# Weight columns side by side in the second product of an attention and MoE kernel, and its last bank transposed apart

## Chip, core and metric

The kernel runs on one core of a Trainium2 chip. The metric is device time in microseconds (us) of one execution. Timed runs give a median; one more execution was profiled, and its trace is what the rows below come from.

## What is computed

```python
# q, k, v: (8, 8, 576, 64) float32; w_in: (512, 2048); w_out: (2048, 512)
scores = scale * np.matmul(q_c, k_c.transpose(0, 1, 2, 4, 3))   # in chunks of 64 rows, scale 1/8
scores = scores - np.max(scores, axis=-1, keepdims=True)
attn = np.exp(scores)
attn = attn / (np.sum(attn, axis=-1, keepdims=True) + 1e-09)
out = np.matmul(attn, v_c)
...
x = attn_out.transpose(0, 2, 1, 3).reshape(4608, 512)
h = x @ w_in
g = np.where(h >= 1, h, np.where(h <= -1, 0.0, (h + 1) ** 2 / 4))
result = g @ w_out
```

## The kernel before

Everything is computed to fp32 accuracy from fp32r products: each operand is split into a high and a low half, and a product is three matmuls (high x high, low x high, high x low) that add into one PSUM bank. The 4608 tokens lie in nine tiles of 512. The first three tiles go through the two feed-forward products directly (L625 first, L661 second). The other six go in **three pairs**, t = 3, 5 and 7, and each pair uses a seven-product scheme in place of eight block products: a whole stage (`whole_last`, matmuls at L918), where the hidden layer comes from P1 to P7, and an output stage (`both_out`, matmuls at L1124), where the second product comes from another set named P1 to P7. Chunk attention for later tiles is slipped between these products as bursts (L480 scores, L502 values).

**The output stage.** `OUT_ORDER` is P1, P2, P6, P5, P7, P3, P4; each has NQ = 8 steps, 56 steps a pair. A step takes one block of combined weights [128, 512] from a ring (`from_ring`; ten slots, filled from DRAM by DMAs on POOL's queue, `load_next_of_ring`) as its stationary operand, and one block of activations as its moving operand. The activations are prepared by `operand_of`: ACT casts the high half into one of 12 slots (L743), VectorE subtracts to get the low half (L747); some need a VectorE sum first. A step is six matmuls of 128 x 128 by 128 x 512, three into each of two banks. The first three don't need the low half until the third one.

Which bank takes which columns: the weight block is read as `"p (x d b) -> p x b d"`, so bank b gets the columns 2d + b, every second one. A result leaves transposed: VectorE's 32 x 32 transposes write both banks interleaved into one staging buffer (L1155), and four DMAs write rows of 64 floats, 256 bytes, to DRAM (`send`, L1163), on SP's queue, for the very last product two on SP's and two on ACT's.

**Banks.** `o_banks[2:]` are the two halves of one PSUM buffer, `ps_o23`; `o_banks[:2]` and `h_banks` are two separate buffers each. A reader of a buffer waits for all writes to that buffer that stand ahead of it. In each pair P1, P6, P7 and P4 run on the halves of `ps_o23`, P2 on `h_banks`, P5 and P3 on `o_banks[:2]`. The whole stage uses `h_banks` and `o_banks[:2]` in turn.

**The end.** For the last product of the last pair (P4) the last `LAST` = 3 steps are emitted together and bank by bank: all of bank 0, then all of bank 1.

**What sets the order.** Every piece is given to a `Plan` with an engine, a cost and its keys; `Plan.emit` walks a modelled time and emits the pieces in the order in which each engine would take them. So the order is fixed at build time, and each engine runs its own list in that order. DMAs from SP and ACT take eight semaphore lanes in turn (DMAHW0 to DMAHW7), and one that takes a lane waits until the DMA before it on that lane has landed. The staging buffers of a pair's first two sends are also the place of a later operand (`take_low`: `low`), which may be written once the sends have left.

The places that matter, L1085 and L1122:

```python
        banks = dict(zip(OUT_ORDER, (o_banks[2:], h_banks, o_banks[2:], o_banks[:2], o_banks[2:], o_banks[:2],
                                     o_banks[2:])))
...
                        w = ap().rearrange("p (x d b) -> p x b d", x=2, b=2)
```

## Time and profile before

| | us |
|---|---|
| median of 3 timed runs | 816.32 (814.77 to 816.89) |
| the profiled execution | 815.4 |
| its span in the trace | 813.6 |
| the output stages: first, second, third pair | 404 to 490, 571 to 653, 726 to 807 |

The span is what the trace covers, from the first to the last instruction. TensorE's granted clock is 0.998 of full over the span. Names in the rows: PE is TensorE's matmuls, PEld its weight loads (they run beside matmuls), DVE is VectorE, ACT ScalarE, SPq and ACTq are the DMA issues of SP and ACT. Buffers that were handed on show the name of the tile that lies there: `new_wi` and `new_wo` are places of former weights that hold the operands, blocks and ring slots of the pairs. A row of a timeline begins with its start and its length in us; neighbouring instructions of one form are merged, and their count stands behind the x.

### The profile page before, as it was taken

The numbers are of one execution on the slowest core, as the hardware profiler recorded it, in microseconds if no ns is written. First come the engines' busy times: TensorE is split into PE (matmuls) and PEld (weight loads), VectorE is DVE, ScalarE is ACT, GpSimd is POOL, SyncE is SP. The second block draws the span as 40 slices with busy tenths as digits, with TensorE's granted clock in tenths as the row PEclk, the third lists the DMA queues.
The fourth block names the chain that finished last, engine by engine and source line by source line (L and its number), as shares of the span: only waits on it lengthen the run. The fifth ranks groups of instructions, "written<-read, shape, count | busy, mean of one in ns | idle before, by whom it ended". The sixth has DMA issues, their size and how long they took to land.

```text
span 813.6 us, 16852 instructions
## 1 busy us (share of the span) xinstructions
PE 800.5 (98%) x5648; PEld 657.0 (81%) x5648; DVE 656.4 (81%) x1131; ACT 538.9 (66%) x1293; POOL 343.1 (42%) x606
## 2 busy tenths in 40 slices
PE   8999999999999999999999999999999999999996
PEld 7778778888888888888888888888888888888885
DVE  5899998768799996776999995877995845589851
ACT  5799876555577675687985655888854456685440
POOL 2112223575655464554554334554333333333330
PEclk9999999999999999999999999999999999999999
DMA  9999725887988897999999788977676886666773
GB/s 216 250 272 271 212 50 150 242 272 226 288 253 228 203 295 197 292 259 253 255 257 269 207 239 254 258 225 210 181 215 188 220 236 194 195 193 191 213 204 88
DMA packets 264149, 181.50 MB, mean 223 GB/s; under 512 B 217600, under 2 KB 229376, under 8 KB 264064
## 3 DMA queue, kind: packets, MB, share of 16 engines
q0 software_dynamic: 40640, 122.72, 48.3%
q1 hardware_dynamic: 220256, 56.92, 31.9%
q10 hardware_dynamic: 3168, 0.79, 0.5%
q8 instruction: 45, 0.74, 0.4%
q14 instruction: 40, 0.33, 0.1%
HBM read 133.17 MB, written 38.80 MB: 211 GB/s over the span
## 4 chain that ended last, share of the span: by engine, by line
PE 87%; DMA 4%; DVE 4%; SPq 4%; issue 1%; ACT 0%; DVEq 0%; ACTq 0%
PE ps_o L1124 25%; PE ps_o L918 14%; PE ps_h L918 14%; PE ps_o L661 13%; PE ps_h L625 13%; PE ps_h L1124 4%; PE ps_a L502 2%; DMA q_sb<-in_q_dram 2%; PE ps_a L480 2%; SPq L382 1%; DMA words<-in_moe_w_in_dram 1%; DVE parts L350 1%; SPq L368 1%; DMA k_sb<-in_k_dram 1%; SPq L388 1%
## 5 line engine op out<-in xcount | busy, mean ns | idle before, releaser
L743 ACT CAST new_wi<-new_wi 128x512 fp32r<-128x512 f32 x157 | 94.9, 626 | 64.8 <-PE ps_o L1124 34.7
L747 DVE TENSOR_TENSOR new_wi<-new_wi,new_wi 128x512 fp32r<-128x512 f32 (+2 forms) x191 | 122.1, 674 | 15.3 <-ACT new_wi L743 12.1
L625 PE MATMUL ps_h<-xh,parts 128*128 128x512 f32 x384 | 130.0, 398 | 2.6 <-DVE r L636 1.4
L661 PE MATMUL ps_o<-parts,gh 128*128 128x512 f32 x384 | 118.5, 390 | 0.0
L625 PEld LDWEIGHTS ps_h<-xh,parts 128*128 128x128 f32 x384 | 71.9, 188 | 19.5 <-DVE parts L350 2.1
L580 POOL DMA_DIRECT2D aT<-e x96 | 48.3, 510 | 87.3 <-ACT tmp L323 34.3
L661 PEld LDWEIGHTS ps_o<-parts,gh 128*128 128x128 f32 x384 | 71.9, 188 | 14.9
L661 PE MATMUL ps_o<-parts,gl 128*128 128x512 f32 x192 | 74.7, 389 | 0.0
L949 DVE SCALAR_TENSOR_TENSOR new_wi<-h,new_wi 128x512 f32<-128x512 f32 x63 | 42.3, 684 | 26.1 <-ACT new_wi L948 26.1
L547 ACT ACTIVATE e<-ps_a,mx 128x64 f32<-128x64 f32 x168 | 50.8, 327 | 10.5 <-DVE mx L541 5.4
L948 ACT ACTIVATE new_wi<-new_wi 128x512 f32<-128x512 f32 x84 | 51.2, 627 | 1.2
L945 ACT ACTIVATE new_wi<-h 128x512 f32<-128x512 f32 x63 | 39.5, 632 | 17.0 <-DVE h L939 17.0
L625 PE MATMUL ps_h<-x_parts,parts 128*128 128x512 f32 x128 | 50.1, 391 | 0.2 <-DVE x_parts L610 0.2
L644 ACT CAST gh<-r 128x512 fp32r<-128x512 f32 x48 | 29.9, 622 | 27.6 <-DVE r L636 19.5
L1124 PE MATMUL ps_o<-new_wi,new_wo 128*128 128x512 f32 x180 | 44.6, 394 | 0.0
L1124 PE MATMUL ps_o<-new_wi,ring_gh 128*128 128x512 f32 x168 | 43.8, 395 | 0.0
L1124 PE MATMUL ps_o<-new_wi,ring_gl 128*128 128x512 f32 x168 | 43.8, 395 | 0.0
L661 PEld LDWEIGHTS ps_o<-parts,gl 128*128 128x128 f32 x192 | 36.1, 188 | 7.5
L1124 PE MATMUL ps_o<-new_wi,ring_r 128*128 128x512 f32 x168 | 41.6, 394 | 0.0
L1124 PEld LDWEIGHTS ps_o<-new_wi,new_wo 128*128 128x128 f32 x180 | 34.7, 193 | 7.2
L1124 PE MATMUL ps_o<-new_wi,new_wi 128*128 128x512 f32 x162 | 40.4, 394 | 0.0
L747 DVE TENSOR_TENSOR new_wi<-new_wi 128x512 f32<-128x512 f32 (+2 forms) x64 | 39.5, 632 | 0.5
(229 smaller groups left out, 2034.4 us busy)
## 6 DMA issues: line engine op xcount, KB each, us to landing
ring_r<-combos POOLq DMA_DIRECT2D x36, 256.0 KB, 3.8
new_wo<-sums_P POOLq DMA_DIRECT2D x36, 256.0 KB, 3.1
new_wi<-combos POOLq DMA_DIRECT2D x34, 256.0 KB, 4.0
new_wi<-sums_P POOLq DMA_DIRECT2D x34, 256.0 KB, 3.2
ring_gh<-combos POOLq DMA_DIRECT2D x33, 256.0 KB, 4.1
ring_gl<-combos POOLq DMA_DIRECT2D x33, 256.0 KB, 4.3
ring_gh<-sums_P POOLq DMA_DIRECT2D x33, 256.0 KB, 3.4
ring_gl<-sums_P POOLq DMA_DIRECT2D x33, 256.0 KB, 3.4
```

The costliest lines, as they stand in the source:

```text
L547: nc.scalar.activation(out=e3[:, n, :], in_=sc[:, n // 4, n % 4, :], func=AF.Exp, bias=mx[:, n, :], scale=SCALE, accum_out=sm[:, n, :],)
L580: queues[queue].dma_start(out=aT[b:b + Q, to], in_=x[a:a + Q, of])
L625: nc.tensor.matmul(out=ps, lhsT=weight["wi", j][:, half, kc * P:(kc + 1) * P], rhs=x, start=(kc == 0 and i == 0), stop=(kc == KC - 1 and i ...
L644: plan.add("act", 0.52, lambda: nc.scalar.copy(out=gh, in_=now(r)), (rkey,), (ghkey, f"split_{t}_{j}"), ahead=ahead)
L661: nc.tensor.matmul(out=acc, lhsT=x[:, cols], rhs=weight["wo", j][:, half, :], start=(j == 0 and i == 0), stop=(j == NF - 1 and i == 2),)
L743: "act", cost, lambda: nc.scalar.copy(out=out(), in_=src()), reads, writes, ahead=ahead
L747: plan.add("dve", cost, lambda: nc.vector.tensor_tensor(out=out(), in0=one(), in1=two(), op=op), reads, writes, port=True, ahead=ahead)
L918: nc.tensor.matmul(out=ps, lhsT=w()[:, at:at + P], rhs=y(), start=name in FRESH and i == 0 and k == 0, stop=i == 1 and k == 2, skip_group_ ...
L945: plan.add("act", 0.52, lambda: nc.scalar.activation(out=now(r), in_=h(), func=AF.Relu, bias=0.5, scale=0.5), (hkey,), (rkey,), ahead=50)
L948: plan.add("act", 0.52, lambda: nc.scalar.square(out=now(r), in_=now(r)), (), (rkey,), ahead=50)
L949: plan.add("dve", 0.6, lambda: nc.vector.scalar_tensor_tensor(out=now(r), in0=h(), scalar=1.0, in1=now(r), op0=ALU.max, op1=ALU.min), (hke ...
L1124: nc.tensor.matmul(out=acc, lhsT=w[:, half, b], rhs=x(), start=name in alone and p == 0 and k == 0, stop=p == NQ - 1 and k == 2, skip_grou ...
```

## The change

- The weight block is read as `"p (x b d) -> p x b d"`: bank b gets the 128 columns b x 128 to b x 128 + 127, which lie side by side.
- So a bank holds whole output columns in one block, the transposes write each bank to its own contiguous half of the staging buffer, and a DMA writes rows of 32 floats, 128 bytes. A send is eight DMAs in place of four, four for each bank, and those of a bank depend on that bank's transpose alone.
- In the last pair P1, P6, P7 and P4 run on `h_banks` (two buffers), P2 on the halves of `ps_o23`. The other pairs keep their banks.
- `LAST` is 4: the last four steps of the last product go bank by bank.

```diff
-        banks = dict(zip(OUT_ORDER, (o_banks[2:], h_banks, o_banks[2:], o_banks[:2], o_banks[2:], o_banks[:2],
-                                     o_banks[2:])))
+        run, other = (h_banks, o_banks[2:]) if last else (o_banks[2:], h_banks)
+        banks = dict(zip(OUT_ORDER, (run, other, run, o_banks[:2], run, o_banks[:2], run)))
...
-                        w = ap().rearrange("p (x d b) -> p x b d", x=2, b=2)
+                        w = ap().rearrange("p (x b d) -> p x b d", x=2, b=2)
...
             for b, (key, ap) in enumerate(source):
-                plan.add("dve", 0.62, lambda b=b, ap=ap: nc.vector.transpose(
-                    out=turned().rearrange("p (n d b) -> p b n d", b=2, d=Q)[:, b],
-                    in_=ap().rearrange("p (n d) -> p n d", d=Q),
-                ), (key,), (keys[b],), ahead=0 if last else -40)
-            for n, queue in enumerate(queues_of):
-                def emit(n=n, queue=queue):
+                plan.add("dve", 0.62, lambda b=b, ap=ap: nc.vector.transpose(out=room_of()[:, b, :], in_=ap()),
+                         (key,), (keys[b],), ahead=0 if last else -40)
+
+                def emit(n, queue, b=b):
                     for a in range(n, P // Q, len(queues_of)):
-                        d = half * QC + a * 2 * Q
+                        d = half * QC + b * P + a * Q
                         queues[queue].dma_start(
-                            out=out[row:row + T, d:d + 2 * Q].rearrange("(n p) d -> p n d", p=Q),
-                            in_=turned()[a * Q:(a + 1) * Q].rearrange("p (n d) -> p n d", d=2 * Q),
+                            out=out[row:row + T, d:d + Q].rearrange("(n p) d -> p n d", p=Q),
+                            in_=room_of()[a * Q:(a + 1) * Q, b].rearrange("p (n d) -> p n d", d=Q),
                         )
 
-                plan.add(queue, 2.6 / len(queues_of), emit, keys, (), lag=1.7, moving=2.6 / len(queues_of))
+                for n, queue in enumerate(queues_of):
+                    plan.add(queue, 2.6 / len(queues_of), lambda n=n, queue=queue, emit=emit: emit(n, queue),
+                             (keys[b],), (), lag=1.7, moving=1.7 / len(queues_of))
...
-    LAST = 3
+    LAST = 4
```

The order of instructions changes in a few places; POOL's doesn't. First TensorE's list at its end, the grouped steps of P4 in the last pair. In the kernel before, where `ps_o_135` is the buffer with both halves:

```order
L1124 MATMUL ps_o_135<-new_wi_8_3113,new_wi_9_3174 128x512 [waits DMASW1_49,Activation_49]
L1124 MATMUL ps_o_135<-new_wi_8_3113,new_wi_9_3174 128x512
L1124 MATMUL ps_o_135<-new_wi_8_3113,new_wi_9_3174 128x512 [waits DVE_49]
L1124 MATMUL ps_o_135<-new_wi_5_2883,ring_r_3681 128x512 [waits DMASW2_49,Activation_49]
L1124 MATMUL ps_o_135<-new_wi_5_2883,ring_r_3681 128x512
L1124 MATMUL ps_o_135<-new_wi_5_2883,ring_r_3681 128x512 [waits DVE_49]
L1124 MATMUL ps_o_135<-new_wi_8_3113,ring_r_3693 128x512 [waits DMASW3_49,Activation_49]
L1124 MATMUL ps_o_135<-new_wi_8_3113,ring_r_3693 128x512
L1124 MATMUL ps_o_135<-new_wi_8_3113,ring_r_3693 128x512 [waits DVE_49]
L1124 MATMUL ps_o_135<-new_wi_8_3113,new_wi_9_3174 128x512 x3
L1124 MATMUL ps_o_135<-new_wi_5_2883,ring_r_3681 128x512 x3
L1124 MATMUL ps_o_135<-new_wi_8_3113,ring_r_3693 128x512 x3
```

And in the changed kernel, where `ps_h_139` is bank 0 and `ps_h_140` bank 1:

```order
L1124 MATMUL ps_h_139<-new_wi_5_2883,ring_r_3681 128x512 [waits DMASW2_49,Activation_49]
L1124 MATMUL ps_h_139<-new_wi_5_2883,ring_r_3681 128x512
L1124 MATMUL ps_h_139<-new_wi_5_2883,ring_r_3681 128x512 [waits DVE_49]
L1124 MATMUL ps_h_139<-new_wi_8_3113,ring_r_3693 128x512 [waits DMASW3_49,Activation_49]
L1124 MATMUL ps_h_139<-new_wi_8_3113,ring_r_3693 128x512
L1124 MATMUL ps_h_139<-new_wi_8_3113,ring_r_3693 128x512 [waits DVE_49]
L1124 MATMUL ps_h_140<-new_wi_4_2806,new_wi_9_3174 128x512 x3
L1124 MATMUL ps_h_140<-new_wi_8_3113,new_wi_9_3174 128x512 x3
L1124 MATMUL ps_h_140<-new_wi_5_2883,ring_r_3681 128x512 x3
L1124 MATMUL ps_h_140<-new_wi_8_3113,ring_r_3693 128x512 x3
```

Twelve matmuls, not nine, now follow the last one of bank 0, and they write another buffer.

Second, the last DMAs. SP's list in the kernel before ends with the send of P3 (`new_wi_16_3682`) and half of that of P4 (`new_wi_12_3409`); the other half is ACT's, on the lanes 7 and 1:

```order
L1163 DMA out_dram<-new_wi_16_3682 32x16x64 [waits DMAHW4_49,DVE_49]
L1163 DMA out_dram<-new_wi_16_3682 32x16x64 [waits DMAHW5_49]
L1163 DMA out_dram<-new_wi_16_3682 32x16x64 [waits DMAHW6_49]
L1163 DMA out_dram<-new_wi_16_3682 32x16x64 [waits DMAHW0_49]
L1163 DMA out_dram<-new_wi_12_3409 32x16x64 [waits DMAHW2_49,DVE_49]
L1163 DMA out_dram<-new_wi_12_3409 32x16x64 [waits DMAHW3_49]
```

SP's list in the changed kernel, from the second bank of P3's send on:

```order
L1158 DMA out_dram<-new_wi_16_3682 32x16x32 [waits DMAHW1_49,DVE_49]
L1158 DMA out_dram<-new_wi_16_3682 32x16x32 [waits DMAHW3_49]
L1158 DMA out_dram<-new_wi_16_3682 32x16x32 [waits DMAHW5_49]
L1158 DMA out_dram<-new_wi_16_3682 32x16x32 [waits DMAHW7_49]
L1158 DMA out_dram<-new_wi_12_3409 32x16x32 [waits DMAHW0_49,DVE_49]
L1158 DMA out_dram<-new_wi_12_3409 32x16x32 [waits DMAHW1_49]
L1158 DMA out_dram<-new_wi_12_3409 32x16x32 [waits DMAHW2_49,DVE_49]
L1158 DMA out_dram<-new_wi_12_3409 32x16x32 [waits DMAHW3_49]
```

ACT's list in the changed kernel ends with its share of P4's send:

```order
L743 CAST new_wi_8_3113<-new_wi_14_3582 128x512 [waits DVE_49,PE_49]
L1158 DMA out_dram<-new_wi_12_3409 32x16x32 [waits DMAHW0_49,DVE_49]
L1158 DMA out_dram<-new_wi_12_3409 32x16x32 [waits DMAHW2_49]
L1158 DMA out_dram<-new_wi_12_3409 32x16x32 [waits DMAHW4_49,DVE_49]
L1158 DMA out_dram<-new_wi_12_3409 32x16x32 [waits DMAHW6_49]
```

The lanes are handed out in turn over both queues, ACT's four between SP's last four of P3, so that SP's first and third DMA of P4 come second on the lanes 0 and 2, behind ACT's first two.

Third, ACT in the middle of the first pair's output stage, where `low` is the operand that takes the place of the first staging buffer. Before:

```order
L743 CAST new_wi_8_3113<-new_wi_15_3621 128x512 [waits DVE_49]
L743 CAST new_wi_6_2959<-new_wi_10_3333 128x512 [waits PE_49,Activation_49]
L743 CAST low_5132<-raw_2435 128x512 [waits DMAHW2_49,DMAHW3_49,DMAHW1_49,DMAHW0_49]
L743 CAST new_wi_6_2959<-new_wi_11_3334 128x512 [waits PE_49,Activation_49]
L743 CAST new_wi_5_2883<-new_wi_16_3682 128x512 [waits DVE_49]
L743 CAST new_wi_4_2806<-new_wi_12_3409 128x512 [waits PE_49,Activation_49]
```

The same place on ACT in the changed kernel:

```order
L743 CAST new_wi_8_3113<-new_wi_15_3621 128x512 [waits DVE_49]
L743 CAST new_wi_6_2959<-new_wi_10_3333 128x512 [waits PE_49,Activation_49]
L743 CAST new_wi_6_2959<-new_wi_11_3334 128x512 [waits PE_49,Activation_49]
L743 CAST new_wi_5_2883<-new_wi_16_3682 128x512 [waits DVE_49]
L743 CAST low_5147<-raw_2435 128x512 [waits DMAHW4_49,DMAHW5_49,DMAHW3_49,DMAHW6_49,DMAHW2_49,DMAHW7_49,DMAHW1_49,DMAHW0_49]
L743 CAST new_wi_4_2806<-new_wi_12_3409 128x512 [waits PE_49,Activation_49]
```

The cast of `low` moved two places back and waits for eight DMAs in place of four.

## Rows read from the trace of the kernel before

**Rows 1.** The page's engine table: busy us, share of the span, instructions.

```profile
PE 800.5 (98%) x5648; PEld 657.0 (81%) x5648; DVE 656.4 (81%) x1131; ACT 538.9 (66%) x1293; POOL 343.1 (42%) x606
```

**Rows 2.** Chain of waits: the page's shares, then pieces (start us, us, what).

```profile
PE 87%; DMA 4%; DVE 4%; SPq 4%; issue 1%; ACT 0%; DVEq 0%; ACTq 0%
...
652.68 5.44 PE ps_h L918 x24
...
751.27 56.02 PE ps_o L1124 x240
```

**Rows 3.** Groups by line and shape, weight loads: busy us, mean ns, idle before.

```profile
L1124 PEld LDWEIGHTS ps_o<-new_wi,new_wo 128*128 128x128 f32 x180 | 34.7, 193 | 7.2
...
L918 PEld LDWEIGHTS ps_h<-new_wi,ring_gl 128*128 128x128 f32 x114 | 21.2, 188 | 4.5
```

**Rows 4.** Waits of ACT, second pair's output stage: us, times, longest us.

```profile
ACT new_wi L743 <- PE ps_o L1124: 23.1, 27, 3.6
```

**Rows 5.** Busy us by stretch: PE, PEld, DVE, ACT, POOL, clock, DMA share, GB/s.

```profile
416.00:434.00 18.00, 18.00 (x138) 14.76 (x137) 17.89 (x36) 12.19 (x46) 9.58 (x19) 1.00 1.05 263
...
760.00:800.00 40.00, 40.00 (x173) 33.10 (x172) 23.73 (x37) 16.27 (x28) 13.36 (x25) 1.00 0.66 192
```

**Rows 6.** Waits of VectorE and of ACT, 404 to 446 us, longest of each.

```profile
DVE mx L536 <- ACT more L743: 0.5, 1, 0.5
...
ACT new_wi L743 <- DVE new_wi L747: 10.2, 6, 3.9
```

**Rows 7.** Timeline of VectorE and TensorE in the first pair's output stage.

```profile
446.83 0.68 DVE L747 TENSOR_TENSOR new_wi<-new_wi,new_wi 128x512 fp32r<-128x512 f32 x1
...
447.64 2.96 PE L1124 MATMUL ps_o<-new_wi,new_wi 128*128 128x512 f32 x12
```

**Rows 8.** DMA view, 797:803, 463:471, 797:803, 808:814: queue's packets, MB, share; issues' landing us.

```profile
q1 hardware_dynamic: 2112, 0.52, 34.2%
...
q1 hardware_dynamic: 3676, 0.46, 37.1%
...
out_dram<-new_wi SPq DMA_DIRECT2D x4, 128.0 KB, 2.3
...
out_dram<-new_wi ACTq DMA_DIRECT2D x2, 128.0 KB, 3.0
```

**Rows 9.** DMA view, 400 to 450 us: the ring loads that land latest.

```profile
new_wo<-sums_P POOLq DMA_DIRECT2D x7, 256.0 KB, 4.9
```

**Rows 10.** Timelines of SP, ACT and TensorE, around sends of the first pair.

```profile
440.34 2.16 SPq L1163 DMA_DIRECT2D out_dram<-stage  x4
...
447.84 0.62 ACT L743 CAST low<-raw 128x512 fp32r<-128x512 f32 x1 [0.15 <-DMA out_dram<-stage]
...
487.73 2.42 SPq L580 DMA_DIRECT2D aT<-e  x4
...
503.34 0.69 PE L502 MATMUL ps_a<-aT,v_sb 64*64 64x64 f32 x32
```

**Rows 11.** Groups by line and shape, transposes: busy us, mean ns, idle before.

```profile
L456 DVE STREAM_TRANSPOSE kT<-k_sb 128x512 f32<-128x512 f32 x32 | 22.1, 691 | 0.0
...
L1155 DVE STREAM_TRANSPOSE stage<-h 128x512 f32<-128x512 f32 x12 | 8.1, 696 | 0.0
```

**Rows 12.** Timeline where the last pair's output stage begins.

```profile
723.60 0.68 DVE L949 SCALAR_TENSOR_TENSOR new_wo<-ps_h,new_wo 128x512 f32<-128x512 f32 x1
...
725.98 1.56 PE L1124 MATMUL ps_o<-new_wi,new_wo 128*128 128x512 f32 x6
```

**Rows 13.** Timeline of the tail.

```profile
805.71 1.56 PE L1124 MATMUL ps_o<-new_wi,ring_r 128*128 128x512 f32 x6
807.31 1.32 DVE L1155 STREAM_TRANSPOSE new_wi<-ps_o 128x512 f32<-128x512 f32 x2 [9.30 <-PE ps_o L1124]
808.65 0.85 SPq L1163 DMA_DIRECT2D out_dram<-new_wi  x2
```

**Rows 14.** Waits of SP's queue in the tail: us, times, longest us.

```profile
SPq L1431 <- DMA out_dram<-new_wi: 2.6, 1, 2.6
```

More of the change, by code (lines that the diff above doesn't have):

```diff
@@ L1149, in send @@
             row = BATCH[tile] * S
-            def turned():
-                return room_of().rearrange("p x t -> p (x t)")
             for b, (key, ap) in enumerate(source):
-                plan.add("dve", 0.62, lambda b=b, ap=ap: nc.vector.transpose(
-                    out=turned().rearrange("p (n d b) -> p b n d", b=2, d=Q)[:, b],
-                    in_=ap().rearrange("p (n d) -> p n d", d=Q),
-                ), (key,), (keys[b],), ahead=0 if last else -40)
-            for n, queue in enumerate(queues_of):
-                def emit(n=n, queue=queue):
+                plan.add("dve", 0.62, lambda b=b, ap=ap: nc.vector.transpose(out=room_of()[:, b, :], in_=ap()),
+                         (key,), (keys[b],), ahead=0 if last else -40)
+                def emit(n, queue, b=b):
                     for a in range(n, P // Q, len(queues_of)):
-                        d = half * QC + a * 2 * Q
+                        d = half * QC + b * P + a * Q
                         queues[queue].dma_start(
-                            out=out[row:row + T, d:d + 2 * Q].rearrange("(n p) d -> p n d", p=Q),
-                            in_=turned()[a * Q:(a + 1) * Q].rearrange("p (n d) -> p n d", d=2 * Q),
-                        )
-                plan.add(queue, 2.6 / len(queues_of), emit, keys, (), lag=1.7, moving=2.6 / len(queues_of))
+                            out=out[row:row + T, d:d + Q].rearrange("(n p) d -> p n d", p=Q),
+                            in_=room_of()[a * Q:(a + 1) * Q, b].rearrange("p (n d) -> p n d", d=Q),
+                        )
+                for n, queue in enumerate(queues_of):
+                    plan.add(queue, 2.6 / len(queues_of), lambda n=n, queue=queue, emit=emit: emit(n, queue),
+                             (keys[b],), (), lag=1.7, moving=1.7 / len(queues_of))
         for n in range(2):
```

## The prediction

> **What bounds the kernel now.** I read the page's engine table first: TensorE is busy 98% of an 813.6 us span, the next engine 81% [rows 1]. A busy matmul engine proves little, since the ends of matmuls are modelled, so the chain of waits comes next. It is TensorE's own work for 87%, and in the last pair's output it is one unbroken piece of 240 matmuls in 56.02 us [rows 2]. Nobody makes TensorE wait there; a gain must come from the time between its matmuls, or from what stands behind the last one. So I asked how long one takes. In the same view the output products (L1124) run at 56.02 / 240 = 233.4 ns a matmul, and the hidden-layer products of the pairs (L918), with moving operand and output of the same shape, at 5.44 / 24 = 226.7 ns [rows 2]. The groups by line and shape show what goes with it: a weight load of L1124 takes 193 ns, one of L918 188, both 128x128 [rows 3]. L918 and L1124 take their operands from the same tiles; what differs is that L1124's stationary columns lie two elements apart.
>
> **The weight layout.** Three pairs x seven products x eight steps x six matmuls are 1008 matmuls of L1124. At 233.4 - 226.7 = 6.7 ns each that is 6.7 us, all on the path [rows 2]. Bounds: if only the weight load's own 193 - 188 = 5 ns came off, 5.0 us [rows 3]; if the layout has no part in it, 0. I take 6.7, because the spacing is what the chain is made of and every strided load stands at the higher value.
> The Trainium skill speaks against this term. "Advanced Engine Details and Errata", section SBUF Cachelines, has 16-byte lines and full speed as long as two accesses hit each line; two fp32 columns 8 bytes apart do share a line, so by it the layout would cost nothing and the sum would lose its first term. The trace disagrees as far as it reaches: 193 against 188 ns with the stride as the one difference I can find [rows 3].
>
> **Who feeds a faster TensorE.** A step of six matmuls will take 1.36 us in place of 1.40, so each step comes 0.04 us earlier against its feeders than the one before.
> In the second pair ACT's casts of the operands wait 23.1 us for TensorE to free their slots, so they run ahead of it and will move along; the third pair is built alike, and I cost both at nothing [rows 4]. In the first pair VectorE is busy 17.89 of 18 us (416 to 434), and from 404 to 446 it waits 0.5 us for anyone, while ACT waits 10.2 us for VectorE [rows 5, 6]. VectorE is the feeder at its limit there. I followed the low halves to their steps: the tightest is the 27th of the 56, whose low half is ready at 446.83 + 0.68 = 447.51, while its third matmul, the first that needs it, starts at 447.64 + 2 x 0.233 = 448.11 [rows 7]. Cover 0.60 us; 26 steps take 26 x 0.04 = 1.04 us of it. So TensorE waits about **0.5 us** there, with some 0.06 us for the signal. The steps behind have about 0.2 us more cover each and take 0.04, so the wait doesn't repeat. Bounds: 0, and the pair's whole gain, 56 x 0.04 = 2.2 us.
>
> **Twice the output DMAs.** Twelve sends to DRAM go from 2048 packets of 256 B to 4096 of 128 B. The send at 798 us, alone on its queue, shows 34.2% of 16 engines x 6 us / 2112 packets = 15.5 ns a packet; loads in rows of 128 B show 37.1% x 16 x 8 / 3676 = 12.9 ns [rows 8]. No 128-byte write is in the trace; by the nearest rows it costs between 12.9 and 15.5 ns. I take 12.9: a send then costs (4096 x 12.9 - 2048 x 15.5) / 16 = 1.3 us more of all engines, twelve of them 15.8 us (24 with the other price). None is on the path as long as the weight ring keeps its lead: a slot is refilled ten steps (13.6 us) before use, and the loads land after 4.9 us even in the fullest stretch [rows 9]. Each send also holds SP for four more issues of 2.16 / 4 = 0.54 us, 2.2 us in all. Behind one of them in SP's queue stand the moves of aT at 487.73, which TensorE reads at 503.34: hidden, as are the head loads behind others [rows 10].
> One place isn't free. The first pair's low operand is cast by ACT into the buffer that the first send leaves from, and that cast already waits 0.15 us for this send [rows 10]. Now it waits for eight DMAs; the new order puts it two casts later. SP starts after the first transpose, so the last of eight is issued about 1.5 us later than the last of four was and should land near 449.5; the cast, due about 448.9, holds ACT 0.6 us, and behind it stand operands that are due over 2 us later. I add **0.2 us** (0 to 1.0).
>
> **Banks and transposes.** The transposes now write contiguously. Strided ones take 696 ns, the contiguous ones of k 691: no change, cost 0 [rows 11]. The last pair's set moves to ps_h, where its first product now has to wait until the hidden layer's readers are done: the last read ends at 723.60 + 0.68 = 724.28, the product starts at 725.98 [rows 12]. 1.7 us of cover, cost 0; without it TensorE would wait for the rest of that read.
>
> **The tail.** Before, both transposes wait for the last matmul (ends 805.71 + 1.56 = 807.27; VectorE had idled 9.30 us), both banks being one buffer; then the DMAs are issued from 808.65 to 809.50, and SP waits another 2.6 us for them, to about 812.3, 5.0 us behind the last matmul [rows 13, 14]. Now bank 0 is complete 12 matmuls = 2.7 us before the end and is transposed at once. Counting from the new last matmul: bank 0 leaves VectorE at -1.9; ACT issues its two DMAs at -1.9 and -1.5. SP's first may not be issued before ACT's first has landed, since both use semaphore lane 0 (the order in the change). With the 2.3 us that a lone send needs to land, that is at +0.4; SP's four follow at +0.4, +0.8, +1.3 and +1.8 and the last lands at +4.1, against 5.0: about **-1.0 us** [rows 8, 13]. The four steps taken bank by bank need the last step's operands three matmuls (0.7 us) sooner; VectorE's 9.30 us of idling say that they are there, cost 0 [rows 13]. Bank 1, transposed at +0.7, isn't what ends last; SP's queue is. With 3.0 us (ACT's DMAs of the tail) for each landing the last comes at +5.3, 0.3 worse; without the lane's wait at +3.5, some 1.6 better.
>
> **Sum.** -6.7 + 0.5 + 0.2 - 1.0 = -7.0 us. The profiled execution took 815.4 us, 1.8 around its span, so it should become about 808.4. It lies 0.9 under the median of the three timed runs, 816.32; against that the forecast is **809.3 us**.
>
> **Rivals.**
> *VectorE takes the first pair's gain.* If the cover is smaller than I read it, or the cast of the low operand blocks longer, the first pair stays at its old pace: 816.3 - 6.7 + 2.2 - 1.0 = 810.8, with 1 us more for a blocked cast 811.8. For it: VectorE is full for over 40 us. Against: its cover grows behind the 27th step. 0.11.
> *The layout isn't the cause, and the change doesn't do what it says.* Then L1124 keeps 233.4 ns, the feeders see no difference, and only the tail is left: 816.3 - 1.0 = 815.3. Nothing in the rows is for it; they tie the 5 ns to the stride alone [rows 3]. 0.07. The skill's line rule above would give this one. So would "TensorE: Matmul & The Clock Gate", section LDWEIGHTS, which counts columns alone (128 / 1.2 = 107 ns), whatever their distance; neither 188 nor 193 is that.
> *Slower: the small rows starve the ring.* If 128-byte writes crowd the weight loads, TensorE waits for the ring. At most all the added engine time is then on the path: 816.3 - 7.0 + 15.8 = 825. It begins once loads take 13 us to land (13.6 less 0.5 for the issue) in place of 4.9, and makes the kernel slower once more than 7 of the 15.8 us are exposed. Against it: that lead, and a DMA share of 0.66 in the last pair [rows 5, 9]. 0.03.
>
> **How the numbers follow.** Forecast as summed 0.79, first rival 0.11, second 0.07, third 0.03. The likeliest case runs from -8.3 (no stall, best tail) to -4.0 (5.0 us from the layout, stalls 0.7, worst tail), 808.0 to 812.3; the first rival lies inside, and 0.6 us below is for the spread of the timed runs: 807.4 to 812.3. About 0.3% (2.4 us) is what a measurement here can tell from no change; the bound for faster is 813.9. Forecast and first rival lie under it: 0.90. The second gives the same: 0.07. The third slower: 0.03.
>
> **What would show it.** Right: weight loads of the output products at 188 ns and unbroken pieces of 240 matmuls near 54.4 us; a TensorE wait on VectorE of about 0.5 us near the 27th step of the first pair and none in the other two; ring loads still landing in about 5 us; the first transpose of the tail over 2 us before the last matmul's end, SP's last DMA landing about 4 us behind it. Wrong: 193 ns or 233 ns again; waits of TensorE for the ring; a tail of 5 us or more; a wait of several microseconds of ACT for the output DMAs in the first pair.

## The result, and the profile of the changed kernel

| | before | after |
|---|---|---|
| median, six runs each (us) | 815.99 (814.77 to 816.89) | 807.19 (806.63 to 809.29) |
| profiled execution, its span | 815.4, 813.6 | 807.0, 805.3 |

The ratio is 0.990, 95% interval 0.988 to 0.991: faster, by about 1%. The forecast was 809.3 us with a range of 807.4 to 812.3; the direction is the forecast one, and the median lies 0.2 us below the range.

A kernel's time mixes the stages that were changed with a beginning that was not, so the two traces are compared by stage. In the table a stage's length runs from the start of its first matmul of L1124 to the start of its last; the tail runs from the start of the very last matmul to the end of the span. All of them are differences of two start times in the trace.

| us | 1st pair | 2nd pair | 3rd pair | tail |
|---|---|---|---|---|
| before | 84.79 | 80.89 | 80.89 | 6.73 |
| after | 83.22 | 78.65 | 78.68 | 5.30 |
| difference | -1.57 | -2.24 | -2.21 | -1.43 |

The four sum to -7.45 us. The span shrank by 8.35; the other 0.9 us lie ahead of the first output stage, where both kernels run the same instructions (it begins at 404.62 before, 403.73 after). They belong to no edit; the section on what was not expected comes back to them.

Engine table of the changed kernel, which answers to [rows 1]:

```profile
PE 796.5 (99%) x5648; PEld 653.9 (81%) x5648; DVE 655.5 (81%) x1131; ACT 538.0 (67%) x1293; POOL 344.0 (43%) x606
```

TensorE's busy share hardly moves, 98 to 99%: it could not have told that 1% was to be had. The chain of waits and the groups by line and shape tell it (chain: start us, us, what; groups: busy us, mean ns, idle before), against [rows 2, 3]:

```profile
582.68 10.88 PE ps_h L1124 x48
593.56 54.40 PE ps_o L1124 x240
647.96 5.44 PE ps_h L918 x24
```

```profile
L918 PEld LDWEIGHTS ps_h<-new_wi,ring_gl 128*128 128x128 f32 x114 | 21.2, 188 | 4.5
...
L1124 PEld LDWEIGHTS ps_o<-new_wi,new_wo 128*128 128x128 f32 x156 | 29.2, 188 | 6.3 <-DVE new_wi L747 0.3
```

The unbroken piece is now 54.40 / 240 = 226.7 ns a matmul, exactly the spacing of L918, and L1124's weight loads take the same 188 ns. The new entry at the end of that row, 0.3 us of idle time put down to VectorE, is the stall that the prediction expected. The waits of TensorE's weight loads from 396 us on (us, times, longest) and the timeline of the place show it:

```profile
PEld ps_o L1124 <- DVE new_wi L747: 0.8, 2, 0.6
```

```profile
444.87 0.76 PEld L1124 LDWEIGHTS ps_o<-new_wi,new_wo 128*128 128x128 f32 x4 [0.25 <-DVE new_wi L747]
...
446.68 2.15 PEld L1124 LDWEIGHTS ps_o<-new_wi,new_wi 128*128 128x128 f32 x10 [0.58 <-DVE new_wi L747]
```

```profile
445.94 0.69 DVE L747 TENSOR_TENSOR new_wi<-new_wi,new_wi 128x512 fp32r<-128x512 f32 x1
```

The low half of the 27th step is ready at 445.94 + 0.69 = 446.63, and the load that needs it goes 0.05 us later, after 0.58 us of waiting; the step before lost a little too. The other two pairs show no such wait.

ACT's cast of the low operand (timeline), and all its waits for the sends from 396 us on:

```profile
449.55 0.62 ACT L743 CAST low<-raw 128x512 fp32r<-128x512 f32 x1 [1.67 <-DMA out_dram<-stage]
```

```profile
ACT low L743 <- DMA out_dram<-stage: 3.9, 3, 1.7
```

It waits 1.67 us where [rows 10] had 0.15, and twice more elsewhere; no wait of TensorE follows.

The tail, timeline, against [rows 13], and SP's waits from 786 us on, against [rows 14]:

```profile
790.84 11.36 SPq L1158 DMA_DIRECT2D out_dram<-new_wi  x12
...
797.67 0.72 DVE L1152 STREAM_TRANSPOSE new_wi<-ps_h 128x512 f32<-128x512 f32 x1 [6.26 <-PE ps_h L1124]
798.42 3.67 ACTq L1158 DMA_DIRECT2D out_dram<-new_wi  x4
798.83 1.52 PE L1124 MATMUL ps_h<-new_wi,ring_r 128*128 128x512 f32 x6
800.39 0.72 DVE L1152 STREAM_TRANSPOSE new_wi<-ps_h 128x512 f32<-128x512 f32 x1 [2.00 <-PE ps_h L1124]
```

```profile
SPq L1158 <- DMA out_dram<-new_wi: 4.7, 1, 4.7
SPq L1428 <- DMA out_dram<-new_wi: 1.7, 3, 0.8
```

The last matmul ends at 798.83 + 1.52 = 800.35. Bank 0 is transposed 2.7 us before that, and its first DMA goes on ACT's queue at 798.42. The profile puts 4.7 us of SP's idling down to lane 0; bank 0 left VectorE only at 797.67 + 0.72 = 798.39, so the lane alone held SP for 1.9 us. It issues at 800.25, right behind the landing of ACT's first DMA at 800.19. The last DMA lands at 804.11, 3.76 us behind the last matmul, against 5.07 before.

### The profile page after: what moved, and what is told of

The parts are those of the page before. It is cut to its first block, busy times and chain, and to the rows that moved or that the text cites. A ratio compares the mean times of both kernels' runs of the same rounds, so it can differ in the third digit from the quotient of the medians.

```text
span 805.3 us, 16930 instructions
## 1 busy us (share of the span) xinstructions
PE 796.5 (99%) x5648; PEld 653.9 (81%) x5648; DVE 655.5 (81%) x1131; ACT 538.0 (67%) x1293; POOL 344.0 (43%) x606
## 4 chain that ended last, share of the span: by engine, by line
PE 84%; DVE 6%; DMA 5%; ACT 2%; issue 1%; SPq 1%; POOL 1%; DVEq 0%; POOLq 0%
PE ps_o L1124 17%; PE ps_h L625 15%; PE ps_o L661 14%; PE ps_h L918 13%; PE ps_o L918 13%; PE ps_h L1124 7%; PE ps_a L502 2%; DVE new_wi L747 2%; PE ps_a L480 2%; DMA v_sb<-in_v_dram 1%; DMA aT<-e 1%; DMA words<-in_moe_w_in_dram 1%; PE ps_h L1382 1%; DMA q_sb<-in_q_dram 1%; DMA ring_r<-sums_P 1%
## 5 line engine op out<-in xcount | busy, mean ns | idle before, releaser
L547 ACT ACTIVATE e<-ps_a,mx 128x64 f32<-128x64 f32 x168 | 50.8, 327 | 11.5 <-DVE mx L541 4.3
L636 DVE SCALAR_TENSOR_TENSOR r<-ps_h,r 128x512 f32<-128x512 f32 x48 | 32.7, 682 | 7.6 <-ACT r L635 7.6
L632 ACT ACTIVATE r<-ps_h 128x512 f32<-128x512 f32 x48 | 29.2, 608 | 12.9 <-PE ps_h L625 12.7
L1124 PE MATMUL ps_o<-new_wi,new_wo 128*128 128x512 f32 x156 | 37.6, 390 | 0.0
L646 DVE TENSOR_TENSOR gl<-r,gh 128x512 fp32r<-128x512 f32 x48 | 32.7, 684 | 5.5 <-ACT gh L644 5.1
L547 ACT ACTIVATION_READ_ACCUMULATOR e<-ps_a,mx 128x1 f32 x168 | 36.8, 219 | 0.0
L1124 PE MATMUL ps_o<-new_wi,ring_gh 128*128 128x512 f32 x138 | 35.1, 390 | 0.0
```

Of the source, the lines that this page charges most:

```text
L547: nc.scalar.activation(out=e3[:, n, :], in_=sc[:, n // 4, n % 4, :], func=AF.Exp, bias=mx[:, n, :], scale=SCALE, accum_out=sm[:, n, :],)
L636: plan.add("dve", 0.6, lambda: nc.vector.scalar_tensor_tensor(out=r, in0=ps, scalar=1.0, in1=r, op0=ALU.max, op1=ALU.min), (pkey,), (rkey,))
L1124: nc.tensor.matmul(out=acc, lhsT=w[:, half, b], rhs=x(), start=name in alone and p == 0 and k == 0, stop=p == NQ - 1 and k == 2, skip_grou ...
```

## Experiments

Stages of all kernels, in the terms of the table above:

| us | 1st pair | 2nd | 3rd | tail | ratio to before (95%) |
|---|---|---|---|---|---|
| layout alone | 83.21 | 78.65 | 78.65 | 6.72 | 0.993 (0.991 to 0.994) |
| rows and tail, columns two apart | 84.79 | 80.89 | 81.66 | 5.30 | 0.999 (0.998 to 1.000) |
| one buffer | 83.19 | 78.65 | 78.68 | 7.31 | 0.994 (0.992 to 0.995) |
| lane exposed | 83.20 | 78.65 | 78.66 | 6.44 | 0.993 (0.991 to 0.995) |
| columns four apart | 86.04 | 81.47 | 81.47 | 5.33 | one run |
| columns three apart | 85.70 | 81.66 | 81.66 | 5.29 | one run |
| rows of 64 bytes | 93.45 | 84.98 | 78.69 | 10.08 | 1.016 (1.013 to 1.018) |
| transposes later | 83.46 | 78.65 | 78.68 | 5.31 | 0.990 (0.988 to 0.992) |
| less VectorE work | 84.12 | 78.65 | 78.68 | 5.31 | 0.991 (0.989 to 0.993) |
| bank 0 on ACT | 83.21 | 78.65 | 78.68 | 5.30 | 0.992 (0.990 to 0.993) |
| rows, tail and old banks, two apart | 84.79 | 80.89 | 81.66 | 7.29 | one run |
| less VectorE work, cast later | 82.66 | 78.65 | 78.67 | 5.27 | 0.991 (0.989 to 0.993) |

The intervals are about 0.3% wide, 2.4 us; most of the questions below are smaller, so they are settled in the stages and not by the times.

### The layout alone

```diff
-                        w = ap().rearrange("p (x d b) -> p x b d", x=2, b=2)
+                        w = ap().rearrange("p (x b d) -> p x b d", x=2, b=2)
```

in the kernel before, and nothing else.

> The kernel before with the one change that a weight block's 128 columns a bank lie side by side; banks, rows of 256 bytes, sends and the last three steps stay (the output's columns come out in another order inside each half). Theory A, the stride of the stationary operand sets the spacing of the matmuls: weight loads of L1124 at 188 ns, unbroken pieces of 240 matmuls at 54.4 us, 1.5 to 1.6 us less in the first pair's output stage and 2.2 less in each of the others, with a wait of TensorE for VectorE of about 0.6 us near the 27th step of the first pair; from the last matmul to the end of the span 6.3 us as before. 816.0 - 6.1 = 809.9 us. Rival B, the layout has no part in it (two fp32 columns 8 bytes apart share a 16-byte line) and banks, sends and last steps made the gain: loads at 193 ns, pieces at 56.0 us, 816.0 us.

808.87 us. All three stages are those of the changed kernel to 0.03 us, and the tail is that of before: the layout alone gives 1.58 + 2.24 + 2.24 = 6.06 us. The order of the casts and sends is that of the kernel before here, and the stall at the 27th step is there all the same (0.8 us in two waits, the longest 0.6), so it has nothing to do with the doubled DMAs.

### The rest without the layout

The same line turned back in the changed kernel.

> The changed kernel with the weight columns two apart again (the output's columns come out in another order inside each half); rows of 128 bytes, eight DMAs a send, the last pair's banks and the four last steps stay. Theory A: weight loads of L1124 at 193 ns, the output stages as long as before, no wait of TensorE for VectorE near the 27th step, the tail 1.4 us shorter: 816.0 - 1.4 = 814.6 us. Rival B (the layout isn't the cause): 188 ns, 807.2 us. Rival C, the doubled DMAs cost TensorE something that the faster matmuls covered up: the stages longer than before by more than 0.5 us, 815 us or more.

813.86 us against 814.9 for the kernel before in the same series. First two stages as before, tail as after (-1.43): A's shape. But the third pair took 0.77 us more than before, which neither theory had. It isn't a wait; the matmuls there stand 235.6 ns apart on average, in a pattern of 233, 235 and 238. A last run asks whether the banks did it:

```diff
-        run, other = (h_banks, o_banks[2:]) if last else (o_banks[2:], h_banks)
+        run, other = o_banks[2:], h_banks
```

> The changed kernel with the weight columns two apart and the banks of before in the last pair; rows of 128 bytes and the last four steps bank by bank stay (the output's columns come out in another order inside each half). With the columns two apart and the changed banks the third pair's output stage had run at 235.6 ns a matmul, 0.8 us longer than the 233.3 ns of the other pairs. Theory A, that came with the banks: 233.3 ns in all three pairs here, third pair 80.9 us. Rival B, it came with the small rows or the four last steps: 235.6 ns in the third pair again. Rival C, it is a state that a strided stream falls into by chance: either, or another pair has it.

With the old banks the third pair is slow again, and the second is not (chain of waits, pieces of the second and of the third pair):

```profile
595.65 56.00 PE ps_o L1124 x240
...
750.47 56.54 PE ps_o L1124 x240
```

56.54 / 240 = 235.6 ns in the third, 233.3 in the second, in one execution with one layout. So it isn't the banks. In both runs the first step of the third pair still runs at 233.3, and 235.6 holds from the second step to the last. The four last steps come at the stage's end, so they don't bring it on either. Whether the rows or the point at which the stream begins puts a strided stream on 235.6 stays open. With columns side by side the second and third pairs stood at 226.7 in every run, wherever nothing waited.

### Columns four and three apart

```diff
-                        w = ap().rearrange("p (x b d) -> p x b d", x=2, b=2)
+                        w = ap().rearrange("p (d c) -> p c d", c=4)
...
-                                out=acc, lhsT=w[:, half, b], rhs=x(),
+                                out=acc, lhsT=w[:, 2 * half + b], rhs=x(),
```

and with columns taken by `64 * half + b:64 * half + b + 382:3` for three.

> The changed kernel with the stationary columns four elements apart (16 bytes), so that each has a 16-byte line of its own; the products then use the columns in a wrong order and the output's values are not the reference's, the work is the same. After the first runs: 226.7 ns a matmul side by side, 233.3 two apart. Theory A, the price grows with the bytes that a row of the block spans (512, 1024, 2048 bytes: 6.7 ns for each 512 more): 246.7 ns, 20 us over the changed kernel, near 827 us. Rival B, any distance costs the same: 233.3 ns, near 814 us. Rival C, what counts is how many columns share a line, and one a line is the costly case: far above 247 ns, weight loads above 220 ns.

> The changed kernel with the stationary columns three elements apart (12 bytes); the products use overlapping sets of columns, so the output's values are not the reference's, the work is the same. Theory A (6.7 ns for each 512 bytes more that a row spans): 240.0 ns a matmul, near 820.5 us. Rival B, any distance costs the same: 233.3 ns, near 814 us. Rival C, the number of columns a 16-byte line counts: between two apart and four apart, nearer to four, since most lines hold one.

816.37 and 816.27 us; pieces of 240 matmuls and a row of weight loads, first of four apart, then of three apart:

```profile
598.09 56.39 PE ps_o L1124 x240
```

```profile
L1124 PEld LDWEIGHTS ps_o<-new_wi,new_wo 128*128 128x128 f32 x156 | 37.6, 310 | 0.0
```

```profile
597.69 56.53 PE ps_o L1124 x240
```

```profile
L1124 PEld LDWEIGHTS ps_o<-new_wi,new_wo 128*128 128x128 f32 x156 | 36.9, 253 | 0.0
```

| columns apart | weight load (ns) | spacing of matmuls (ns) |
|---|---|---|
| 1 | 188 | 226.7 |
| 2 | 193 | 233.3 (235.6 in some third pairs) |
| 3 | 253 | 235.6 |
| 4 | 310 | 235.0 |

A falls: the price doesn't grow with the distance. B is nearest, any distance costs 7 to 9 ns. C is half right, and in the quantity that doesn't count: the loads themselves do become long where each column has a line of its own, but a load of 310 ns stands in a stream with one matmul every 235 ns, so most of it lies beside other work.

### One buffer at the end

The bank line above, turned back in the changed kernel with its columns side by side.

> The changed kernel with the banks of before in the last pair: P1, P6, P7 and P4 on the two halves of one buffer. Theory A, a reader waits for all writes to the buffer: both transposes start after the last matmul and take 1.4 us, ACT's first two DMAs go at +0.8 and +1.2 from the last matmul's end, SP's second waits on a semaphore lane for ACT's first to land (about +2.6), its last is issued near +3.5 and lands near +5.8, against +3.8 in the changed kernel: 807.2 + 2.0 = 809.2 us. Rival B, without a wait on the lanes: SP's fourth goes at +2.3 and lands at +4.5, 807.9 us. Rival C, bank 0 is released by its own last write, whichever buffer it lies in: transposed 2 us before the end, 807.2 us.

809.95 us. The tail grows by 2.01 us, as A has it. Timeline and SP's waits:

```profile
799.92 1.52 PE L1124 MATMUL ps_o<-new_wi,ring_r 128*128 128x512 f32 x6
...
801.48 1.31 DVE L1152 STREAM_TRANSPOSE new_wi<-ps_o 128x512 f32<-128x512 f32 x2 [8.98 <-PE ps_o L1124]
```

```profile
SPq L1158 <- DMA out_dram<-new_wi: 2.0, 2, 1.8
```

VectorE idles 8.98 us, and both transposes start only when the last matmul has ended (801.44). With one buffer the eight DMAs would have made the tail worse than before (7.31 against 6.73): the new banks aren't an extra, the shorter tail hangs on them.

### The lanes, exposed and removed

```diff
-                    for a in range(n, P // Q, len(queues_of)):
+                    for a in range(n, P // Q, len(queues_of) if b else 1):
...
-                for n, queue in enumerate(queues_of):
+                some = queues_of if b else queues_of[:1]
+                for n, queue in enumerate(some):
...
```

puts bank 0's four DMAs on SP; with `queues_of[-1:]` they go on ACT. Bank 1's are split over both queues each time.

> The changed kernel with the last product's send divided otherwise: bank 0's four DMAs all on SP, bank 1's two on SP and two on ACT. No DMA of bank 0 now waits for ACT, but SP's first of bank 1 comes second on lane 2 behind ACT's first of bank 1, issued at about the same time. Theory A, a lane is taken again only when the DMA before on it has landed: bank 0's four go at -1.9 to -0.4, SP's first of bank 1 not before +0.85 + 2.0 = +2.9, the last lands near +5.4 against +3.8 in the changed kernel: 807.2 + 1.6 = 808.8 us. Rival B, the lanes hold nobody up: SP's two of bank 1 go at +0.8 and +1.2, the last lands at +3.5: 806.9 us.

> The changed kernel with the last product's send divided otherwise again: bank 0's four DMAs on ACT, bank 1's two on SP and two on ACT; every lane that they take is free by then. Theory A: bank 0 goes at -1.9 to -0.4 from the last matmul's end, bank 1 at +0.8 and +1.2 on both queues, the last DMA lands at +3.3 to +3.5 in place of +3.8: 806.8 us. Rival B, SP's wait on ACT's lane in the changed kernel was hidden to the end behind bank 1's transpose, and the last landing hangs on ACT's last issue alone: +3.5 to +3.8, 807.2 us.

809.09 us with bank 0 on SP. SP's first of bank 1 comes second on a lane behind ACT's first of bank 1; it waits for that landing:

```profile
SPq L1158 <- DMA out_dram<-new_wi: 2.6, 1, 2.6
```

The tail is 1.14 us longer than in the changed kernel, A in kind, and 0.5 us smaller than I put it, since a lone DMA lands after 1.77 us and not 2.0 and the last one after 1.9. With bank 0 on ACT no queue waits for a lane, and the tail is 5.30 us, the same to 0.01: B. In the changed kernel SP's wait ends at 800.25 and its two DMAs of bank 0 have just been issued when bank 1 leaves VectorE (800.39 + 0.72 = 801.11), so the wait is hidden to the end; SP's and ACT's first DMAs of bank 1 go at 801.20 and 801.13. The same 1.8 us of landing cost 1.1 us when they stand behind the last transpose, and nothing ahead of it.

### Small rows taken further

Two DMAs of 16 floats a row in place of one of 32, so sixteen a send.

> The changed kernel with rows of 64 bytes: sixteen DMAs a send in place of eight, 8192 packets in place of 4096. Theory A, small rows are hidden as long as the weight ring keeps its lead, and they cost where somebody waits for a send: ring loads land in 4 to 6 us; SP's share of the last product's send is eight DMAs, its last is issued 2 us later, +2.2 us in the tail; the cast of the low operand in the first pair now waits for DMAs that SP needs 8.6 us to issue, about 4 us more, more than the 2 us that the operands behind it have, so 0 to 3 us of TensorE waiting there: 809.4 to 812.5 us. Rival B, doubling the DMAs costs at the buffer alone and nothing else: 809.4 us. Rival C, the rows starve the ring: TensorE waits for ring loads, 815 us or more.

829.48 us, more than A or B said, and not for C's reason. The third pair isn't touched, and the ring's loads land after 3.9 to 5.0 us between 400 and 450 us. Waits from 396 us on, and the timeline of ACT and of TensorE's weight loads near the end of the first pair:

```profile
PEld ps_o L1124 <- ACT new_wi L743: 11.5, 3, 5.9
```

```profile
489.61 0.62 ACT L743 CAST low<-raw 128x512 fp32r<-128x512 f32 x1 [9.25 <-DMA out_dram<-stage]
```

```profile
490.80 0.50 PEld L1124 LDWEIGHTS ps_o<-new_wi,ring_gh 128*128 128x128 f32 x2 [5.86 <-ACT new_wi L743]
```

ACT takes its list in order. Its cast of the low operand waits 9.25 us for sixteen DMAs that SP issues one by one, the operands behind it are late, and TensorE stands still. The first pair grows by 10.2 us and the second by 6.3; the third has no such cast. The waits for ACT are 11.5 us of that. Most of the rest is TensorE's clock, which was granted in full up to there: behind idle stretches of 5.4 and 3.3 us the granted clock is 0.50, the level of 1.2 GHz in place of 2.4, and each time about a dozen matmuls go 427 ns apart in place of 227, some 2.5 us a pair. Stretches ahead of and behind the first of them, columns as in [rows 5]:

```profile
480.00:489.00 9.00, 5.36 (x24) 4.12 (x22) 3.66 (x7) 0.36 (x1) 3.35 (x7) 1.00 1.03 269
490.00:496.00 6.00, 5.20 (x12) 4.01 (x13) 5.67 (x11) 3.03 (x7) 0.54 (x1) 0.50 0.17 19
```

The tail's 4.8 us are the lane once more: twice as many DMAs shift the lanes, and the last of P3's sixteen on SP now comes second on a lane behind one of ACT's for bank 1 of P4.

```profile
SPq L1159 <- DMA out_dram<-new_wi: 4.1, 1, 4.1
```

It goes 2.5 us behind the last matmul, and SP's eight of the last product follow it, 0.5 us each. So the danger of small rows in this kernel lies in the number of issues on one queue and in those who wait for them, and not in the load on the DMA engines.

### Where the stall in the first pair comes from

First the two transposes of the first send moved behind the step that stalls:

```diff
-                         (key,), (keys[b],), ahead=0 if last else -40)
+                         (key,), (keys[b],), ahead=0 if last else -80 if tile == ALONE + 1 and half == 0 else -40)
```

> The changed kernel with one number of the order changed: the two transposes of the first pair's first send stand 18 operations later in VectorE's list (behind the low halves of the steps 27 to 29), and a burst of attention matmuls stands four steps later in TensorE's. Theory A, the wait of 0.6 us at the first pair's 27th step is VectorE's list being full ahead of it: both transposes (1.2 us) gone from in front of it, TensorE's wait there is 0, at the 26th step 0.2 us may stay; the first pair's output stage takes 82.6 to 82.8 us in place of 83.2, 806.7 us. Rival B, the wait comes from ACT or from the cast that waits for the send's DMAs, and VectorE's list has no part in it: 0.6 us stays, 807.2 us. Rival C, what is moved back is late elsewhere: a new wait of TensorE for VectorE behind the 29th step, 807.2 to 808.5 us.

807.99 us, first stage 83.46. The 27th step's wait is gone, and the 26th waits 0.40 us in place of 0.25, with two more of 0.4 us at the steps 53 and 55. With the transposes TensorE's burst of attention products moved from ahead of the 23rd step to behind the 26th, so the steps between came 1.2 us sooner and ate what VectorE had gained. It doesn't tell A from C, and says that a move in one list rarely stays in it. So work was taken away instead of moved:

```diff
-                dve(0.62, ALU.add, ap, ps, ap, (pkey, key), (key,))
+                m = Q if t == ALONE + 1 and name == "P2" else T
+                dve(0.62, ALU.add, *(lambda s=s, m=m: s()[:, :m] for s in (ap, ps, ap)), (pkey, key), (key,))
```

> The changed kernel with two VectorE sums of the first pair cut to 32 of their 512 columns (the sums of P2 that go into the first send, so those output columns lack a part), the order on every engine as it was. About 1.0 us of VectorE's work is gone from in front of the first pair's 27th step, everything behind it stays. Theory A, that step waits because VectorE is full from the stage's start: the wait of 0.6 us and the 0.25 us at the step before are gone, the stage takes 82.6 us in place of 83.2, 806.6 us. Rival B, something else than VectorE's load holds the low half (ACT's casts, the cast that waits for the send): the waits stay, 807.2 us.

807.92 us, first stage 84.12: the waits at the 26th and 27th steps are gone, as A says, and the stage is longer, which nobody expected. New waits stand at the 32nd step:

```profile
452.83 0.62 ACT L743 CAST low<-raw 128x512 fp32r<-128x512 f32 x1 [3.77 <-DMA out_dram<-stage]
```

```profile
455.06 0.30 PEld L1124 LDWEIGHTS ps_o<-new_wi,ring_gl 128*128 128x128 f32 x2 [0.81 <-ACT new_wi L743]
455.79 0.76 PEld L1124 LDWEIGHTS ps_o<-new_wi,ring_gl 128*128 128x128 f32 x4 [0.43 <-DVE new_wi L747]
```

The cast of the low operand, held for 1.67 us in the changed kernel, is held for 3.77 us here. It came due 0.7 us sooner in its stage, and the send landed 1.4 us later, 47.1 us behind the stage's start and not 45.7, though every engine's list is the same; no run shows why it landed later. The steps 53 and 55 wait for VectorE too, 0.4 us each, behind a second such cast that is held 3.4 us; the run before has the same two waits behind a cast held 0.9 us, so they need not be the cast's. If the held cast is what took the gain back, moving it must return it:

```diff
-                             (keys[b],), (), lag=1.7, moving=1.7 / len(queues_of))
+                             (keys[b],), (), lag=5.0, moving=1.7 / len(queues_of))
```

> The kernel of the run with less VectorE work (two sums of the first pair's P2 cut to 32 of 512 columns), with one number of the order's model raised, the time that a send's DMAs need to land (1.7 to 5.0 us): ACT's casts of the low operands go two to four places further back in its list, TensorE's order stays. In the run without this the first pair's wait at the 27th step was gone, but the cast waited 3.8 us for the send, and TensorE then 0.8 us for ACT and 0.4 us for VectorE at the 32nd step; the stage took 84.1 us. Theory A, that blocked cast is what took the gain back: its wait falls under 1.5 us, the waits at the 32nd step are gone, the first pair's output stage takes 82.6 to 82.9 us, 806.6 us. Rival B, the 32nd step waits for a full VectorE or ACT whatever the cast does: the stage stays near 84 us, 808 us.

807.40 us, first stage 82.66, and no wait of TensorE for VectorE or ACT is left in it. The cast now follows operands that are due sooner, and finds the DMAs just landed:

```profile
448.74 0.62 ACT L743 CAST low<-raw 128x512 fp32r<-128x512 f32 x1
```

A on both counts: 84.79 - 82.66 = 2.13 us of the 2.24 that the layout is worth. One thing beside the order differs: the send landed 45.9 us behind the stage's start, 1.1 us sooner than in the run before. At its old place the cast, due at 43.4, would have been held about 2.5 us, an estimate that lies between 2.0 us, which cost nothing with the lane exposed, and 3.8. So the move of the cast and the sooner landing aren't told apart; what the two runs show is that TensorE waits behind a cast held 3.8 us and not behind one that isn't held. What is left out of the computation here is small, but it is needed; no run keeps it and frees a microsecond of VectorE elsewhere. None of the kernels is measurably faster than the changed one.

## Why the prediction was right, step by step

- **The bound and the layout (-6.7).** Right in size and place. Two pairs got the full 2.24 and 2.21 us, the first 1.57 and a stall: 6.0 us net and, with the stall added, 6.6. The layout alone gave 6.06. The rule of the Trainium skill ("Advanced Engine Details and Errata", section SBUF Cachelines) that two hits a line are full speed does not hold for this stationary operand: two a line cost 6.7 ns a matmul. My reason for taking 6.7 and not 5.0 was that the chain is made of spacings; the stride runs bear it out more than I knew, since a load longer by 122 ns costs 8 ns.
- **The stall (+0.5).** Right place and engine; the 26th step lost some too. Removing VectorE's work removed the waits, and the stage with no wait left is 83.22 - 82.66 = 0.56 us shorter, forecast 0.5. It still lacks 0.11 of the 2.24 us, which no wait accounts for. The rival in which VectorE takes the whole 2.2 us didn't come, for the reason given: the steps behind have more cover.
- **The blocked cast (+0.2).** The landing looks right (449.45 in the trace, 449.5 forecast), but the changed kernel's stage begins 0.89 us sooner. Counted from the stage's start the cast came due at 44.15 us, forecast 44.28, and the send landed at 45.72, forecast 44.88. So the landing was 0.8 us late, and the cast was held 1.67 us, not 0.6, and three times, not once. The order doesn't fix this landing: with every list the same up to there it came at 44.0 us with bank 0 on ACT and at 46.0 with the lane exposed, so to hit it would have been luck. Its price was 0: the first stage takes 83.19 to 83.22 us whether this cast waits 2.00 us (lane exposed), 1.67 (the changed kernel) or not at all (layout alone, one buffer, bank 0 on ACT). I had charged part of the wait to TensorE without following the operands behind it to their steps. The cliff is nearer than the zero suggests: TensorE waited 0.8 us behind this cast where it was held 3.8 us, 1.9 us where it was held 4.7 (rows of 64 bytes), and 5.9 us behind a later one held 9.2.
- **Doubled DMAs (0).** Right: stages of the layout alone, with 256-byte rows, and of the changed kernel, with 128, agree to 0.03 us. The price of a packet was near too: in the tail of the changed kernel (797 to 806 us) 2112 packets took 17.5% of 16 engines x 9 us, 11.9 ns, against 12.9. But the cover that I named, the ring's lead, isn't the one that gives way first. Taken one step further, the cast and the lanes did, at 829 us, with the ring untouched.
- **Transposes, ps_h (0).** The transposes take 694 ns, 696 before, and the third pair's stage starts without a wait.
- **The tail (-1.0).** -1.3 from the last matmul to the last landing (5.07 to 3.76), -1.43 to the end of the span. Bank 0's first issue came at -1.93, forecast -1.9. The step that was off is the lane: SP's first went at -0.1 and not at +0.4, since the first DMA of 64 KB landed after 1.77 us and not after the 2.3 that I took, the median of four twice its size [rows 8]. So SP's queue wasn't what ended last, as I had it: its two DMAs of bank 0 were out by then, and bank 1's transpose, at +0.76, released the last four DMAs. I also valued being rid of the lane at 0.6 us; it is worth nothing here.
- **The sum.** -7.0 forecast, -7.45 in the stages: 0.2 of it the cast, 0.4 the tail, 0.2 the other way the first pair. The timed medians differ by 8.8, 1.35 more than the stages. In the two traces 0.9 of it lies ahead of the output stages, where nothing was changed; the rest no trace shows. The forecast was also counted from 816.32, the median of three runs of the kernel before, and over six it is 815.99. So the terms make 0.45 of the 2.1 us between forecast and median, and the rest, which took the median just under the range, is chance: with bank 0 on ACT the stages and the tail are the same, and that kernel came out 6.6 us below the one before in its series (808.88 and 815.47). I had allowed 0.6 us for the spread of the runs, and that was too little.

## What to carry to other kernels

Ask of a bound engine how far apart its instructions start, form by form: two lines of the same shape that differ by 3% are a gain that no wait and no busy share shows. When the bound engine gets faster, follow each feeder to the step with the least cover, and then follow what stands behind every instruction in a strict list that waits for a transfer: a wait that costs nothing today costs all of its growth once the cover is used. Judge edits of a few microseconds by stages of the trace, since the beginning of a kernel can vary by more than they bring.

## What the runs showed of the chip that was not expected

- **A weight load's length isn't its price.** Loads of 188, 193, 253 and 310 ns go with matmuls 226.7, 233.3, 235.6 and 235.0 ns apart. Side by side or not is what counts; how far apart hardly does.
- **A strided stream has more than one pace.** Two apart, the same code ran at 233.3 ns in one stage and 235.6 in another of the same execution, from its second step to its last. The cause stays open.
- **The beginning varies by 3.9 us.** The first matmul of the first whole stage stands behind the same instructions in all fourteen kernels, and starts between 315.80 us (less VectorE work, cast later) and 319.70 (transposes later):

```profile
315.80 0.84 PE L918 MATMUL ps_h<-lows,new_wo 128*128 128x512 f32 x3
```

```profile
319.70 0.84 PE L918 MATMUL ps_h<-lows,new_wo 128*128 128x512 f32 x3
```

From there on the stages repeat to a few hundredths of a microsecond.
